# Block-sparse attention followed by a rational feed-forward layer: the start of the program in another order, a scale of its own for the first chunk, and its sampled key blocks copied by VectorE

## The chip, the cores and the metric

The kernel runs on one core of a Trainium2 chip. The metric is the device time of one execution in microseconds (us). The kernel before took 877.2 us, the median of three runs (875.51 to 879.96).

## What is computed

```python
B, H, S, D = 4, 8, 768, 64            # q, k, v: float32
scores = (q @ k.T) / sqrt(D)          # per batch and head
# a block of 32 queries sees the key blocks: itself and its two neighbours, block 0, block 23,
# and three sampled blocks (sampled_blocks, 24 x 3); blocks 0 and 23 as queries see all
attn = softmax(where(mask, scores, -1e9)) @ v
x = attn.transpose(0, 2, 1, 3).reshape(B * S, H * D)      # 3072 x 512
h = x @ w_in                                              # 3072 x 2048
P = a[0] + a[1]*h + a[2]*h**2 + a[3]*h**3
Q = 1 + abs(b[0])*abs(h) + abs(b[1])*h**2
out = (P / (Q + 1e-6)) @ w_out                            # 3072 x 512
```

The two weights come as float64 and are unpacked on the chip. q and k, and x and `w_in`, are multiplied in float16 as a high and a low part, each after a scale by a power of two that is found from the largest absolute value.

## The kernel before

**Two halves that run into each other.** Attention works by query blocks of 32 rows (function `attention`, "parts" numbered x; a query block that sees all keys has three parts). One part is: scores on TensorE (PE, L913), maxima on VectorE (DVE, L923), exponentials on ScalarE (ACT, L941), transposes on PE (L982) and their copy out of PSUM (`pT`, L150), products with v on PE (L1039). Four parts make a group: it is weighted (`xn`, L1073), turned (L1085, `xt`), and split into a high part `xh` (`evac_high`, L150 under `times`) and a low part `xl` (L1097). Eight query blocks make a chunk c of 256 rows of x; there are 12 chunks. The feed-forward half works by units (c, u), 8 per chunk: products with `w_in` (L1150 to L1152), the rational function on ACT and DVE, and products with `w_out` (L1206 to L1208). A unit needs its chunk's `xh` and `xl`, and the piece of the weights that it reads.

**The weights.** `weights` loads 16 tiles of `w_in` and 16 of `w_out` of 512 KB through two buffers (`wl`, L435 and L438). Each is converted (L154 or L150) and packed by DVE in three steps (L447, L450, L453). Four tiles make one group of `w_in`: ACT finds the largest value of each (L397), `w_scaled` makes the scale `scw`, and POOL (GpSimd) and ACT make the float16 parts (L154, L150, L511). A group serves two units.

**The first batch.** Its keys lie in SBUF (`kall`). `prep(0, ...)` loads k, bounds it (L397), splits it (L391), turns it on PE and evacuates it into `kall` (L150, L152); it also loads all of v for the bound that gives `v_scale[0]` and `kv[0][4]`, the factor by which x of batch 0 is scaled. For each part with samples, ACT copies three blocks of `kall` to `kx` (L866), at positions that it reads into registers with `TENSOR_LOAD` (L803): one such load brings the numbers of up to four query blocks, three each. SP (SyncE), which issues all DMAs, does the same for the rows of v (L1009). POOL copies the edge blocks into `kx` once (L1109). `prep_q` loads and splits four blocks' queries (`ldq`, L728).

**The order.** A planner (`issue`) places every operation by hand-set priorities and prices and by rings of buffers; each engine then runs its own list strictly in that order, so that an instruction that waits holds up all that stand behind it. Where PE would be idle early on, the planner adds products of the identity that nothing reads (`fill`, L162).

```python
lambda w, stage, j: (-83.96, -78.19)[w] + stage * 0.5                    # when(0): k first, then v
a = Op(SC, 1100, copies, [o_setup, chain["edges"]], p - 1, takes=[s_kx], uses=s_kall)
times(eng, x_part(0), G["xt"], kv[b][4] if plain else 1.0)              # x of a chunk, by v's scale
```

Of the kernel before, what the change touches and what calls it, by code (L numbers as in the profile page):

```python
# [23 lines left out]
def kernel(  # L24
# [265 lines left out]
    ix = const.tile([1, NB, 4], I32, name="ix")  # L290

# [122 lines left out]
    def weights():  # L414
# [5 lines left out]
        for u in range(NG):  # L420
            pieces += [(min(place[0, 2 * u], place[1, 2 * u]) + -4.91, 0, u, x) for x in range(NCC)]
# [131 lines left out]
    def prep(b, when):  # L553


        kv[b] = [None] * 5
        s_scr[b] = Slot(r_ks)
        first = b == 0
        n = len(units)
        k_done[b], v_done[b] = [], []  # L560
        before = {}
        if first:
            rings = [[(r_tt, "tt", p2), (r_ab, "ab", p2), (r_sq, "sq", p2)], [(r_pr, "pr", p3), (r_ld, "ld", p3)]]
        for w in ([2] if b >= QB else []) + [0, 1]:
# [7 lines left out]
            for j in range(n):  # L572
                def one(j, w=w, lds=lds, mx_tile=mx_tile):
                    prio = when(w, 0, j)
                    if first:
                        ring, tag, pool = rings[w][j // (2 + w)]
                    else:
                        ring = r_ld
# [6 lines left out]
                    def load():  # L585
                        if first:
                            nb = {"tt": 3, "pr": 4}.get(tag)
                            d["ld"] = pool.tile([P, 512], F32, name=tag, bufs=nb)
                            if w:
                                nc.sync.dma_start(out=d["ld"], in_=v[b].rearrange("h (a r) d -> (h a) (r d)", a=P // H)[:, j * 512:(j + 1) * 512])  # L590
                            else:
                                load_unit(k, b, *units[j], d["ld"])
# [120 lines left out]
    def prep_q(b, t, prio, before):  # L713
# [4 lines left out]
        s_ld, s_hl, s_ps = Slot(r_ldq), Slot(r_hlq), Slot(r_sp)  # L718
# [4 lines left out]
        def load():  # L723
            d["ld"] = p1.tile([P, 512], F32, name="ldq")
# [58 lines left out]
        x = Op(TE, 445, transposes, [l], prio, takes=[s_ps], uses=[s_hl])  # L783
        x = Op(SC, 904, evac, [x], prio, takes=[d["slot"]], uses=[s_ps])
# [12 lines left out]
    def sampled_rows(x, eng=mybir.EngineType.SP):  # L797

        b, j = parts[x][:2]
        i = block(j)  # L800
        if (b, i, eng) not in rows_of:
            some = [n for n in (block(m) for m in range(j - j % 4, j - j % 4 + 4)) if n not in (0, NB - 1)]
            values = nc.values_load_multi_w_load_instructions(  # L803
                ix[0:1, some[0]:some[-1] + 1, 0:NR], engines=[eng], min_val=0, max_val=NB - 1,
                skip_runtime_bounds_check_because="clamped when ix was written")[1]
            for n, m in enumerate(some):
                rows_of[b, m, eng] = values[n * NR:(n + 1) * NR]
        return rows_of[b, i, eng]
# [19 lines left out]
    xs_of, s_xs, o_ready = {}, {}, {}  # L828
# [4 lines left out]
    def attention(b, j, prio):  # L833
# [8 lines left out]
        if e4 == 0:  # L842
            x_group[w] = {"s_xn": Slot(r_xn), "s_ps": Slot(r_sp), "s_sm": Slot(r_sm), "ops": [], "av": []}
# [5 lines left out]
        for m, x in enumerate(xs):  # L849
            def one(m, x):  # L850
# [9 lines left out]
                elif near:  # L860
                    s_kx = Slot(r_kx)

                    def copies():
                        rows = sampled_rows(x, mybir.EngineType.Activation)
# [104 lines left out]
        for m, x in enumerate(xs):  # L969
            def two(m, x):  # L970
# [72 lines left out]
                ol = chain["vg"] = Op(SY, price, load, [o_setup] + v_done[b],  # L1043
# [36 lines left out]
        s_xn, s_ps = G["s_xn"], G["s_ps"]  # L1080

        def turn_x():
            G["xt"] = ps_s.tile([P, 512], F32, name="sp")
            for e in range(XB):
                nc.tensor.transpose(G["xt"][:, e * P:(e + 1) * P], G["xn"][:, e].rearrange("p g d -> p (g d)"), ident)  # L1085

# [3 lines left out]
        def evac_high(eng):  # L1090
            if c not in xs_of:
                xs_of[c] = xbufs[s_xs[c].buf]
            times(eng, x_part(0), G["xt"], kv[b][4] if plain else 1.0)

        def evac_low():
            if plain:
                nc.vector.scalar_tensor_tensor(out=x_part(1), in0=G["xt"], scalar=kv[b][4], in1=x_part(0), op0=ALU.mult, op1=ALU.subtract)  # L1097
            else:
                nc.vector.tensor_tensor(out=x_part(1), in0=G["xt"], in1=x_part(0), op=ALU.subtract)

        a = chain["xt"] = Op(TE, 435, turn_x, G["ops"], p, takes=[s_ps], uses=[s_xn], behind=chain.get("xt"))
        new = e2 < XB
        a = chain["ev"] = Op(among("v", SC, sc=520, ve=598), 0, evac_high, [a] + ([v_scale[b]] if plain else []), p, behind=chain.get("ev"), takes=[s_xs[c]] if new else [], uses=[s_ps] + ([] if new else [s_xs[c]]))
# [7 lines left out]
    last_near = []  # L1111
    XB = 4
# [4 lines left out]

    def factors(b, u, n, after, prio):

        def run():  # L1120
            if b not in fcs:
                fcs[b] = p2.tile([P, 4, NU], F32, name="fc")
            nc.vector.scalar_tensor_tensor(out=fcs[b][:, :, u:u + n], in0=wscale[:, u:u + n].rearrange("p (o n) -> p o n", o=1).broadcast_to([P, 4, n]), scalar=kv[b][3],
# [9 lines left out]
    def unit(c, u):  # L1133
# [6 lines left out]
        def into(e):  # L1140
            def run():
                xh, xl = xs_of[c]
                d["cst"] = fcs[b][:, :, u]
# [80 lines left out]
        deps = (o_ready[c] + [o_fc[b, u]] if u == 0 else [o_fc[b, u]]) + (in_ready[u * CH // WC] if c < 2 else [])  # L1224
# [81 lines left out]
    def when(b):  # L1306
        if b == 0:
            return lambda w, stage, j: (-83.96, -78.19)[w] + stage * 0.5
# [4 lines left out]
    prep(0, when(0))  # L1313
# [3 lines left out]
    for b in range(B):  # L1317
        if b:
            prep(b, when(b))
        for t in range(NT):  # L1320
            x0 = min(x for x, p in enumerate(parts) if p[0] == b and p[1] // TB == t)
            before = prep_q(b, t, -78.95 if b == t == 0 else part_prio(x0) - (3.23 if x0 >= need[0] else 12.17), before)
# [4 lines left out]
    for c, u in order:  # L1327
        b = c // NCH
        if b == 0 and u % (WC // CH) == 0 and (b, u) not in o_fc:
            factors(0, u, WC // CH, [scale_ready[u * CH // WC], v_scale[0], o_setup], place[c, u] - 1)  # L1330
        elif b and (b, u) not in o_fc:
# [45 lines left out]
```

## Time and profile before

| | |
|---|---|
| median of three runs | 877.2 us (875.51 to 879.96) |
| the profiled execution: its own time | 878.83 us |
| its span, first to last instruction | 877.0 us |
| PE, DVE, ACT, POOL busy | 825.4, 729.0, 675.4, 111.4 us |
| mean granted TensorE clock | 0.976 of full speed |
| moved by DMA | 151.16 MB, 172 GB/s over the span |

Read it by stages, not by the shares: PE's 825.4 us contain the `fill` products of the start, and the bound is not the same engine throughout. "Idle before" is the time in which an engine had nothing running, put down to the instruction that then came and to what released it. Register instructions such as `TENSOR_LOAD` are not counted as busy, so an engine that is held by them looks idle.

### The profile page before, as it was taken

Reading aid. Unit: us, or ns where it says so; the run is one execution under the profiler, and the core shown is the slowest. Engines: PE = TensorE matmul, PEld = TensorE weight load, DVE = VectorE, ACT = ScalarE, POOL = GpSimd, SP = SyncE. Lnnn points to the kernel's source line nnn. Section 1 sums busy time; section 2 is a strip of 40 time slices with the busy share of each in tenths; the row PEclk is TensorE's granted clock in tenths of the full one; section 3 lists DMA queues with packets and bytes.
Section 4 is the critical chain, followed back from the end, with each engine's and each line's share of the span. In section 5 each row is a group of like instructions: output and inputs, shape, how many; then the busy total and the mean of one; then the engine's idle time right before and its main releaser. Section 6 shows DMA issues by size and latency. Waiting matters only on the chain.

```text
span 877.0 us, 27047 instructions
## 1 busy us (share of the span) xinstructions
PE 825.4 (94%) x10334; PEld 644.6 (73%) x10334; DVE 729.0 (83%) x1731; ACT 675.4 (77%) x1447; POOL 111.4 (13%) x118
## 2 busy tenths in 40 slices
PE   8988687588899999999999999999999999999997
PEld 3545566366687888888788887878778888788886
DVE  5758987999998888888887877887878887778886
ACT  6777977797787897798777788998768687767563
POOL 1124622635220000000000000000000000000000
PEclk9999898699999999999999999999999999999999
DMA  7888689586765965889755976899555965630000
GB/s 201 209 158 209 194 177 199 127 238 196 203 156 152 273 203 157 210 214 241 200 146 139 241 204 190 198 248 248 152 131 162 224 170 160 183 102 26 1 25 25
DMA packets 240209, 151.16 MB, mean 172 GB/s; under 512 B 16208, under 2 KB 222928, under 8 KB 240080
## 3 DMA queue, kind: packets, MB, share of 16 engines
q1 hardware_dynamic: 240080, 149.43, 66.4%
q8 instruction: 82, 1.34, 0.7%
q14 instruction: 47, 0.39, 0.2%
HBM read 132.07 MB, written 11.01 MB: 163 GB/s over the span
## 4 chain that ended last, share of the span: by engine, by line
PE 69%; DVE 9%; DMA 9%; ACT 5%; SPq 4%; issue 3%; POOL 1%; ACTq 0%; DVEq 0%; POOLq 0%
PE acc L1206 9%; PE ph L1150 9%; PE acc L1208 8%; PE acc L1207 8%; PE ph L1152 8%; PE ph L1151 8%; PE av L1039 5%; PE pt L982 5%; PE sp L913 5%; DMA vg<-in_v_dram 2%; DMA wl<-in_moe_w_in_dram 2%; ACT pr L941 1%; DVE pr L923 1%; SPq L1009 1%; PE sp L758 1%
## 5 line engine op out<-in xcount | busy, mean ns | idle before, releaser
L1150 PE MATMUL ph<-xh,wi 128*128 128x256 f16 x768 | 212.1, 276 | 3.7 <-DVE tt L1167 3.6
L1152 PE MATMUL ph<-xh,wi 128*128 128x256 f16 x768 | 210.9, 275 | 0.5 <-POOL wi L511 0.5
L1151 PE MATMUL ph<-xl,wi 128*128 128x256 f16 x768 | 210.9, 275 | 0.0
L1206 PE MATMUL acc<-wo_h,gh 128*128 128x512 f32 x376 | 161.2, 429 | 1.4 <-ACT wo_h L150 1.4
L1208 PE MATMUL acc<-wo_h,gl 128*128 128x512 f32 x376 | 151.2, 402 | 2.6 <-DVE gl L1195 2.6
L1207 PE MATMUL acc<-wo_l,gh 128*128 128x512 f32 x376 | 150.5, 400 | 1.5 <-POOL wo_l L464 1.5
L1174 DVE SCALAR_TENSOR_TENSOR ab<-sq,absb,ab 128x512 f32<-128x512 f32 x96 | 73.0, 760 | 51.4 <-ACT ab L1171 51.2
L1157 ACT ACTIVATE sq<-ph,fc 128x512 f32<-128x512 f32 x96 | 65.7, 684 | 63.8 <-PE ph L1152 63.3
L1150 PEld LDWEIGHTS <-wi 128*128 128x128 f16 x768 | 75.7, 99 | 28.8 <-issue 16.3
L923 DVE CUSTOM_DVE_ANT_1 pr<-sp,bias 128x256 f32<-128x256 f32 x224 | 84.6, 418 | 13.3 <-PE sp L913 11.5
L941 ACT ACTIVATE pr<-pr,st,cqb 128x256 f32<-128x256 f32 x112 | 66.1, 593 | 29.1 <-DVE st L952 29.0
L1208 PEld LDWEIGHTS acc<-wo_h,gl 128*128 128x128 f32 x376 | 71.9, 191 | 20.3 <-DVE gl L1195 3.0
L1206 PEld LDWEIGHTS acc<-wo_h,gh 128*128 128x128 f32 x376 | 72.2, 192 | 17.8 <-ACT wo_h L150 1.6
L1185 DVE SCALAR_TENSOR_TENSOR gh<-tt,par,rr 128x512 fp32r<-128x512 f32 x96 | 73.2, 763 | 13.9 <-PE acc L1207 11.2
L982 PE MATMUL pt<-ident,pr 128*128 128x128 f32 x448 | 76.5, 292 | 8.6 <-ACT pr L941 6.9
L1151 PEld LDWEIGHTS <-wi 128*128 128x128 f16 x768 | 75.7, 99 | 11.7 <-issue 3.8
L1039 PE MATMUL av<-vg,pT 128*32 128x64 f32 x3584 | 74.1, 224 | 10.2 <-DMA vg<-in_v_dram 6.2
L1152 PEld LDWEIGHTS <-wi 128*128 128x128 f16 x768 | 75.7, 99 | 10.3 <-POOL wi L511 1.0
L982 PEld LDWEIGHTS pt<-ident,pr 128*128 128x128 f32 x448 | 67.7, 205 | 20.2 <-ACT pr L941 10.1
L1207 PEld LDWEIGHTS acc<-wo_l,gh 128*128 128x128 f32 x376 | 72.3, 192 | 13.8 <-POOL wo_l L464 1.8
L1039 PEld LDWEIGHTS av<-vg,pT 128*32 128x32 f32 x3584 | 56.3, 111 | 35.2 <-issue 15.3
L150 ACT ACTIVATE pT<-pt 128x512 f32<-128x512 f32 x112 | 66.3, 592 | 15.3 <-PE pt L982 13.6
(167 smaller groups left out, 1663.3 us busy)
## 6 DMA issues: line engine op xcount, KB each, us to landing
vg<-in_v_dram SPq DMA_DIRECT2D x312, 64.0 KB, 3.3
vg<-in_v_dram SPq DMA_DIRECT2D x88, 192.0 KB, 3.7
vg<-in_v_dram SPq DMA_DIRECT2D x24, 512.0 KB, 5.5
kall<-ks SPq DMA_DIRECT2D x52, 192.0 KB, 3.3
kall<-ks SPq DMA_DIRECT2D x156, 64.0 KB, 2.2
ld<-in_k_dram SPq DMA_DIRECT2D x36, 256.0 KB, 4.5
wl<-in_moe_w_in_dram SPq DMA_DIRECT2D x32, 256.0 KB, 4.5
wl<-in_moe_w_out_dram SPq DMA_DIRECT2D x16, 512.0 KB, 5.0
```

Source lines behind the costliest of these rows:

```text
L923: nc.vector.tensor_tensor_reduce(out=prs[x][:, g].rearrange("p (s r) -> p s r", r=BLK), in0=h["sp"][:, g].rearrange("p (s r) -> p s r", r= ...
L941: nc.scalar.activation(out=prs[x][:, g], in_=prs[x][:, g], func=AF.Exp, scale=Q["first"]["c"], bias=st[:, 6 + g:7 + g], accum_out=total if ...
L982: nc.tensor.transpose(pp[:, jj * P:(jj + 1) * P], cols, ident)
L1039: nc.tensor.matmul(av[rows, g], pT[:, 2 * g + kt, rows] if plain else pT[:, 2 * g + kt, pa_, rows], vf[:, g * HG + h4, kt * D:(kt + 1) * D ...
L1150: nc.tensor.matmul(o, wh, xh[:, :, cc], start=(cc == 0), stop=False)
L1151: nc.tensor.matmul(o, wh, xl[:, :, cc], start=False, stop=False)
L1152: nc.tensor.matmul(o, wl, xh[:, :, cc], start=False, stop=(cc == NCC - 1))
L1174: nc.vector.scalar_tensor_tensor(out=d["ab"], in0=d["sq"], scalar=absb[:, 1:2], in1=d["ab"], op0=ALU.mult, op1=ALU.add)
L1185: nc.vector.scalar_tensor_tensor(out=d["gh"], in0=d["tt"], scalar=par[:, 0:1], in1=d["rr"], op0=ALU.add, op1=ALU.mult)
L1206: nc.tensor.matmul(acc[:, t], ghs, wo_h[:, f], start=(new and e == 0), stop=False)
L1207: nc.tensor.matmul(acc[:, t], ghs, wo_l[:, f], start=False, stop=False)
L1208: nc.tensor.matmul(acc[:, t], gls, wo_h[:, f], start=False, stop=(last and e == 1))
```

## The change

Six edits, made together:

- **Loads.** v of batch 0 is no longer loaded right after k. Its priority goes from -78.19 to -7.0, and it stands behind the v rows of the last part of chunk 0. The second piece of q is loaded right after the first (it takes a buffer of another ring for that), and the first group of `w_in` gets priority -60.
- **The scale of chunk 0.** x of chunk 0 waits for v's bound no more. Both groups of it stay in PSUM (in the `ph` ring) while ACT finds each one's largest value; a scale `scx` is made of them (one more transpose on PE and five small steps on DVE), and both are then split. Chunk 0 gets its own unit factors (`fc`).
- **The copies of chunk 0.** The sampled blocks of the first eight parts are copied by DVE, those of the other 14 parts of batch 0 by ACT as before.
- **Reading the positions.** The three numbers of a query block are packed into one by DVE at the start; each part loads that one number and takes it apart with register instructions. This holds for all parts, on SP too.
- **Prices** in the planner's table: 700 for three copies on DVE, 1500 on ACT (1100 before); one slot of the q ring is taken earlier.
- Later chunks keep v's scale.

```diff
+        for r in range(NR - 1, 0, -1):
+            nc.vector.scalar_tensor_tensor(out=ix[:, :, NR:NR + 1] if r == 1 else ix[:, :, r - 1:r], in0=ix[:, :, r:r + 1], scalar=float(1 << IXB), in1=ix[:, :, r - 1:r], op0=ALU.mult, op1=ALU.add)
...
-            pieces += [(min(place[0, 2 * u], place[1, 2 * u]) + -4.91, 0, u, x) for x in range(NCC)]
+            pieces += [((min(place[0, 2 * u], place[1, 2 * u]) + -4.91) if u else -60.0, 0, u, x) for x in range(NCC)]
...
+        before = dict.fromkeys(range(3), vg_load.get(need[0] - 1)) if b < 2 else {}
...
-        s_ld, s_hl, s_ps = Slot(r_ldq), Slot(r_hlq), Slot(r_sp)
+        s_ld, s_hl, s_ps = Slot(r_ld if (b, t) == (0, 1) else r_ldq), Slot(r_hlq), Slot(r_sp)
...
-        if (b, i, eng) not in rows_of:
-            some = [n for n in (block(m) for m in range(j - j % 4, j - j % 4 + 4)) if n not in (0, NB - 1)]
...
+        if (x, eng) not in rows_of:
+            n = nc.values_load_multi_w_load_instructions(
+                ix[0:1, block(parts[x][1]), NR:NR + 1], engines=[eng], min_val=0, max_val=(1 << NR * IXB) - 1,
...
+            rows_of[x, eng] = [nc.s_assert_within((n >> r * IXB) & ((1 << IXB) - 1), min_val=0, max_val=NB - 1,
...
-                            nc.scalar.copy(out=kxs[:, s_kx.buf, r].rearrange("p h r -> p (h r)"), in_=kall[:, bass.ds(rows[r], 1)].rearrange("p o h r -> p (o h r)"))
+                            times(nc.vector if dve else nc.scalar, kxs[:, s_kx.buf, r].rearrange("p h r -> p (h r)"), kall[:, bass.ds(rows[r], 1)].rearrange("p o h r -> p (o h r)"), 1.0)
...
-                    a = Op(SC, 1100, copies, [o_setup, chain["edges"]], p - 1, takes=[s_kx], uses=s_kall)
+                    a = Op(VE if dve else SC, 700 if dve else 1500, copies, [o_setup, chain["edges"]], p - 1, takes=[s_kx], uses=s_kall, behind=chain.get("kx"))
...
+        def most():
+            if not x_own:
+                x_own.extend([p4.tile([P, 8], F32, name="mx", bufs=5), p4.tile([P, 1], F32, name="xs0", bufs=1)])
+            bound(G["xt"], x_own[0][:, e2 // XB:e2 // XB + 1])
...
+        o = Op(VE, 75, largest, [w[3] for w in x_wait], p)
+        o, _ = scales(lambda: x_own[0][:, 6:7], "scx", [o], p, finish=keep, keep=lambda s, inv: x_own.append(inv))
+        x_scaled.append(o)
+        for G, e2, p, _ in x_wait:
+            evacuate(G, c, e2, p, x_own, 1, o)
...
-            return lambda w, stage, j: (-83.96, -78.19)[w] + stage * 0.5
+            return lambda w, stage, j: (-83.96, -7.0)[w] + stage * 0.5
...
-            before = prep_q(b, t, -78.95 if b == t == 0 else part_prio(x0) - (3.23 if x0 >= need[0] else 12.17), before)
+            before = prep_q(b, t, -78.95 + 8 * t if b == 0 and t < 2 else part_prio(x0) - (3.23 if x0 >= need[0] else 12.17), before)
```

How the lists move, at three places. First the DMA queue of SP after the last loads of k; `ldq` and `ld` take q, `pr` and `ld` took v, `wl` takes weights, `vg` the v rows of part 0. Before:

```order
L545 DMA sq<-in_k_dram 128x4x128 x2
L728 DMA ldq<-in_q_dram 64x4x128 x2
L590 DMA pr<-in_v_dram 128x512 x3
L590 DMA ld<-in_v_dram 128x512 x3
L1003 DMA vg_110<-in_v_dram 48x8x128
```

and now:

```order
L548 DMA sq<-in_k_dram 128x4x128 x2
L728 DMA ldq<-in_q_dram 64x4x128 x2
L728 DMA ld<-in_q_dram 64x4x128 x2
L441 DMA wl<-in_moe_w_in_dram 64x1024 x4
L1001 DMA vg_110<-in_v_dram 48x8x128
```

The six loads of v have gone from here (they come after the v rows of part 7), and the second piece of q and two tiles of weights stand in their place.

Second, DVE's list just ahead of the first maxima (the ISA rows on `pr,st`). Before:

```order
L365 TENSOR_SCALAR scq<-scq 128x1
L746 SCALAR_TENSOR_TENSOR cq<-scq,sc_259 128x1
L749 TENSOR_SCALAR cq<-cq 128x1
L752 TENSOR_SCALAR cq<-cq 128x1
L391 SCALAR_TENSOR_TENSOR hlq<-ldq,scq,hlq 128x8x64
L923 ISA pr,st<-sp,bias 128x256
```

and now:

```order
L450 TENSOR_SCALAR wi<-wi 128x512
L752 TENSOR_SCALAR cq<-cq 128x1
L453 SCALAR_TENSOR_TENSOR wi<-wl,wi 128x512
L800 TENSOR_LOAD ix
L152 REGISTER_ALU
L152 ISA
L152 COPY kx<-kall 128x256
L152 REGISTER_ALU x2
```

Packing of weights (`wi`) has come ahead of the first maxima, and so have the copies of parts 0 and 1, each part with a load, five register operations, three ISA rows and three copies.

Third, DVE's list where chunk 0's second group is weighted (`xn`) and split (`xl`). Before:

```order
L1073 TENSOR_TENSOR xn<-av,sm 128x512
L749 TENSOR_SCALAR cq<-cq 128x1
L752 TENSOR_SCALAR cq<-cq 128x1
L154 TENSOR_SCALAR wi<-wl 128x512
L447 TENSOR_SCALAR wi<-wi 128x512
L1097 SCALAR_TENSOR_TENSOR xl_116<-sp,xscale,xh_115 128x512
```

and now:

```order
L1071 TENSOR_TENSOR xn<-av,sm 128x512
L1094 TENSOR_REDUCE mx<-mx 128x1
L356 TENSOR_REDUCE scx<-sp 128x1
L359 TENSOR_SCALAR scx<-scx 128x1
L368 TENSOR_SCALAR scx<-scx 128x1
L1097 COPY xs_1066<-scx 128x1
L1152 SCALAR_TENSOR_TENSOR fc<-wscale,scx,coef 128x4x2
L450 TENSOR_SCALAR wi<-wi 128x512
L453 SCALAR_TENSOR_TENSOR wi<-wl,wi 128x512
L1125 SCALAR_TENSOR_TENSOR xl_116<-ph,xs_1066,xh_115 128x512 x2
```

Between weighting and splitting there is now the making of a scale (two of its rows, L363 and L367, are left out here), and both groups are split together.

## Rows read from the trace of the kernel before

**Rows 1.** The span in 40 equal slices of 21.9 us: busy tenths of PE and of DVE (9 is 90% or more).

```profile
PE   8988687588899999999999999999999999999997
...
DVE  5758987999998888888887877887878887778886
```

**Rows 2.** Stretches between 12 and 250 us: length, busy time (and count) of PE, weight loads, DVE, ACT and POOL, granted clock, DMA share, GB/s.

```profile
12.20:30.40 18.20, 17.46 (x151) 9.35 (x152) 14.07 (x43) 13.70 (x32) 5.25 (x8) 1.00 0.68 186
30.40:60.00 29.60, 24.76 (x514) 14.97 (x517) 18.67 (x64) 24.59 (x72) 2.72 (x4) 1.00 0.95 200
60.00:75.00 15.00, 14.71 (x139) 8.34 (x139) 11.46 (x25) 10.06 (x24) 9.57 (x10) 0.89 0.89 175
75.00:100.00 25.00, 18.48 (x355) 12.11 (x352) 21.66 (x64) 21.67 (x54) 14.32 (x13) 1.00 0.70 204
100.00:160.00 60.00, 45.37 (x753) 35.93 (x753) 50.71 (x132) 46.95 (x114) 19.86 (x20) 0.85 0.81 178
160.00:210.00 50.00, 39.83 (x437) 30.86 (x437) 50.00 (x106) 44.55 (x98) 25.84 (x23) 0.84 0.76 202
210.00:250.00 40.00, 34.00 (x452) 26.95 (x452) 39.51 (x93) 29.67 (x61) 12.86 (x12) 0.96 0.70 183
```

**Rows 3.** The `TENSOR_LOAD` of positions (L803): duration in ns (shortest, median, longest), first and last start. The first two rows are of the whole span, the third of 42 to 55 us (a load of twelve numbers), the last of 55 to 75 us (a load of nine: one of the four query blocks has no samples).

```profile
L803 SPq TENSOR_LOAD <-ix x24: 1907/2529/2726, 13.8 to 739.9; - x24
L803 ACTq TENSOR_LOAD <-ix x6: 1991/2659/2836, 25.2 to 151.8; - x6
...
L803 SPq TENSOR_LOAD <-ix x1: 2552/2552/2552, 43.8 to 43.8; - x1
...
L803 SPq TENSOR_LOAD <-ix x1: 1911/1911/1911, 60.4 to 60.4; - x1
```

**Rows 4.** The copies on ACT and their register instructions (L866): duration in ns (shortest, median, longest), first and last start.

```profile
L866 ACTq FUSED_REGOPS  x66: 46/46/52, 28.1 to 157.9; - x66
L866 ACT COPY kx<-kall x66: 386/400/410, 28.2 to 161.1; 128x256 f16 x66
```

**Rows 5.** Groups of DVE and ACT instructions in the first 300 us: line, engine, operation, tiles, shape, count, busy us, mean ns, idle before and its releasers.

```profile
L93 DVE CAST ident<-ident 128x128 f16<-128x128 f32 x1 | 0.2, 227 | 1.4 <-POOL ident masks.py:199 1.4
L333 DVE TENSOR_SCALAR bias<-rr 128x24 f32<-128x24 f32 x3 | 0.3, 184 | 0.1
L152 DVE COPY kall<-ph 128x512 f16<-128x512 f16 x6 | 4.1, 712 | 0.2 <-ACT kall L150 0.2
L353 DVE TENSOR_REDUCE scw<-sp 128x1 f32<-128x128 f32 x4 | 1.1, 284 | 0.1
L356 DVE TENSOR_SCALAR scw<-scw 128x1 f32<-128x1 f32 x4 | 0.6, 143 | 0.0
L1123 DVE SCALAR_TENSOR_TENSOR fc<-wscale,sc,coef 128x8 f32<-128x8 f32 x4 | 1.5, 364 | 0.0
L397 ACT ACTIVATE scrap<-ldq 128x512 f16<-128x512 f32 x10 | 6.3, 629 | 1.7 <-DMA ldq<-in_q_dram 1.7
```

**Rows 6.** The start in order of time: start us, duration us, engine, line, operation, tiles, shape, count, idle before.

```profile
25.23 0.73 ACT L150 ACTIVATE kall<-ph 128x512 f16<-128x512 f16 x1 [0.57 <-PE ph L683]
26.79 1.16 POOL L1109 COPY kx<-kall 128x512 f16<-128x512 f16 x2 [4.74 <-DVE kall L152]
28.23 1.94 ACT L866 COPY kx<-kall 128x256 f16 x6 [2.27 <-DVE cq L752]
29.77 0.23 PE L913 MATMUL sp<-kall,qa 128*32 128x96 f16 x4
...
59.91 0.91 PE L1039 MATMUL av<-vg,pT 128*32 128x64 f32 x32 [3.48 <-DMA vg<-in_v_dram]
61.71 2.03 POOL L154 TENSOR_SCALAR dw<-wi,scw 128x512 f32<-128x512 f32 x3 [12.43 <-DVE scw L365]
66.64 0.74 DVE L1097 SCALAR_TENSOR_TENSOR xl<-sp,xscale,xh 128x512 f16<-128x512 f32 x1
71.21 1.32 POOL L511 TENSOR_TENSOR wi<-dw,wi 128x512 f16<-128x512 f32 x1 [0.23 <-ACT wi L150]
72.47 0.27 PE L1150 MATMUL ph<-xh,wi 128*128 128x256 f16 x1
```

**Rows 7.** Whom DVE waited for: waiting instruction, releaser, us in total, times, longest. The first three rows are of 30.5 to 60 us, the other three of 100 to 160 us.

```profile
DVE wi L447 <- ACT wi L150: 3.3, 1, 3.3
DVE pr L923 <- PE sp L913: 3.0, 3, 1.3
DVE pr L923 <- ACT kx L866: 1.6, 1, 1.6
...
DVE wi L447 <- POOL wi L154: 3.0, 3, 2.0
DVE sums L490 <- ACT scrap L397: 1.8, 1, 1.8
DVE dw L447 <- POOL dw L154: 1.3, 2, 0.8
```

**Rows 8.** The chain that ended last, in order of time, three of its long pieces between 121 and 153 us: start us, length us, what.

```profile
121.13 4.84 DMA wl<-in_moe_w_in_dram
125.98 6.15 DMA wl<-in_moe_w_in_dram
...
144.58 7.48 DMA wl<-in_moe_w_out_dram
```

More of the change, by code (lines that the diff above doesn't have):

```diff
@@ L574, in one @@
                     prio = when(w, 0, j)
-                    if first:
-                        ring, tag, pool = rings[w][j // (2 + w)]
+                    if first and w == 0:
+                        ring, tag, pool = rings[j // 2]
                     else:
@@ L585, in load @@
                     def load():
[L586 to L592, printed above, removed]
+                        if first and w == 0:
+                            d["ld"] = pool.tile([P, 512], F32, name=tag, bufs=3 if tag == "tt" else None)
+                            load_unit(k, b, *units[j], d["ld"])
                         else:
@@ L782, in prep_q @@
             d["first"], d["oc"] = qt[b, 0], qt[b, 0]["oc"]
-        x = Op(TE, 445, transposes, [l], prio, takes=[s_ps], uses=[s_hl])
-        x = Op(SC, 904, evac, [x], prio, takes=[d["slot"]], uses=[s_ps])
+        x = Op(TE, 445, transposes, [l], prio, takes=[s_ps, d["slot"]], uses=[s_hl])
+        x = Op(SC, 904, evac, [x], prio, uses=[s_ps, d["slot"]])
         d["oq"] = Op(SY, [(650, 131072)] * 2, swap, [x], prio, uses=[d["slot"]])
@@ L797, in sampled_rows @@
     def sampled_rows(x, eng=mybir.EngineType.SP):
-        b, j = parts[x][:2]
-        i = block(j)
-        if (b, i, eng) not in rows_of:
-            some = [n for n in (block(m) for m in range(j - j % 4, j - j % 4 + 4)) if n not in (0, NB - 1)]
[L803 to L808, printed above, removed]
+        if (x, eng) not in rows_of:
+            n = nc.values_load_multi_w_load_instructions(
+                ix[0:1, block(parts[x][1]), NR:NR + 1], engines=[eng], min_val=0, max_val=(1 << NR * IXB) - 1,
+                skip_runtime_bounds_check_because="made of numbers clamped when ix was written")[1][0]
+            rows_of[x, eng] = [nc.s_assert_within((n >> r * IXB) & ((1 << IXB) - 1), min_val=0, max_val=NB - 1,
+                                                  skip_runtime_bounds_check_because="clamped when ix was written") for r in range(NR)]
+        return rows_of[x, eng]
     def vrows(vg, kt, slot, n=1):
@@ L1041, in values @@
                                                  start=(n_ == 0 and (n == 1 or (m == 0 and g == 0))), stop=(m == n - 1 and n_ == len(steps) - 1), skip_group_check=n > 1)
-                ol = chain["vg"] = Op(SY, price, load, [o_setup] + v_done[b],
+                ol = chain["vg"] = vg_load[x] = Op(SY, price, load, [o_setup] + v_done[b],
                                       prio[m] - 0.72, takes=[s_vg], uses=[] if plain else [s_scr[b]], behind=chain.get("vg"))
@@ L1092, in evac_high @@
                 xs_of[c] = xbufs[s_xs[c].buf]
-            times(eng, x_part(0), G["xt"], kv[b][4] if plain else 1.0)
+            times(eng, x_part(0), G["xt"], of[n])
         def evac_low():
[L1096 to L1101, printed above, removed]
+            nc.vector.scalar_tensor_tensor(out=x_part(1), in0=G["xt"], scalar=of[n], in1=x_part(0), op0=ALU.mult, op1=ALU.subtract)
         new = e2 < XB
-        a = chain["ev"] = Op(among("v", SC, sc=520, ve=598), 0, evac_high, [a] + ([v_scale[b]] if plain else []), p, behind=chain.get("ev"), takes=[s_xs[c]] if new else [], uses=[s_ps] + ([] if new else [s_xs[c]]))
+        a = chain["ev"] = Op(among("v", SC, sc=520, ve=598), 0, evac_high, [G["turned"], ready], p, behind=chain.get("ev"), takes=[s_xs[c]] if new else [], uses=[s_ps] + ([] if new else [s_xs[c]]))
         l = Op(VE, 602, evac_low, [a], p, uses=[s_ps, s_xs[c]])
@@ L1327 @@
     for c, u in order:
[L1328 to L1331, printed above, removed]
+        b = key(c)
+        if c < 2 and u % (WC // CH) == 0:
+            factors(b, u, WC // CH, [scale_ready[u * CH // WC], v_scale[0] if c else x_scaled[0], o_setup], place[c, u] - 1)
+        elif b > 0 and (b, u) not in o_fc:
             factors(b, 0, NU, [scale_ready[g] for g in range(NG)] + [v_scale[b]], place[c, u] - 2)
```

62 lines of the change are left out of this document (42 added, 20 removed).

## Prediction

> **What bounds the kernel now.** I read the slices first, to see where time is lost. After slice 12 PE shows nines to its last slice; all gaps lie in the first 250 us [rows 1]. In those 250 us the digits of PE also count products that nothing reads, so that I go on by DVE. The stretches show it [rows 2]: between 160 and 250 us DVE is busy for 89.5 of 90 us while PE has 16.2 us idle, so there DVE is the bound. From 12 to 160 us DVE is idle for 31.5 us: 4.1, 10.9, 3.5, 3.3 and 9.3 us, stretch by stretch (length less busy time). DVE's work up to the point at which PE takes over is nearly fixed: splits, packing of weights, maxima, the first units. So the rule for the sum is: **the end moves by what DVE's early work grows, less what is taken out of DVE's idle time before 160 us.** PE is full afterwards and keeps the shift.
>
> Next, who made DVE wait [rows 7]. Between 30 and 60 us it is a conversion of weights that waits for its load and holds up DVE's list (3.3 us), scores (3.0 us) and ACT's copies (1.6 us). Between 100 and 160 us it is conversions and bounds of weights once more, and the long pieces of the chain there are loads of weights of 4.84, 6.15 and 7.48 us [rows 8]: the two `wl` buffers circulate too slowly.
>
> Last, the start in order of time [rows 6]. Keys are in place for POOL's edge copy at 26.79 us, ACT's copies begin at 28.23, the first scores at 29.77. Chunk 0's last `xl` starts at 66.64, but the first unit starts at 72.47, right after the last float16 part of the weights (POOL, 71.21 + 1.32): now weights end last there, not x.
>
> **The change part by part.**
>
> *Register loads.* A load of twelve numbers took 2.55 us, one of nine 1.91 us [rows 3]: 0.21 us for a number, and next to nothing beside it. One number then costs some 0.27 us. To it come five register operations and three address instructions of about 0.046 us each, by the nearest register row [rows 4], 0.37 us: 0.64 us for a part. The load may also have a fixed part that two sizes don't show; the ends are 0.2 us and 1.91 us, the shortest that ran. I take 0.27, since the two sizes lie on a line through nearly zero. The Trainium skill, "DMA: Bandwidth & Descriptors", section "Latency and other measured facts", gives a floor of about 600 ns for a `tensor_load`. By it the eight parts on DVE would cost 2.6 us more in all (8 x 0.33) and the forecast would be near 875; no run so far shows a load of one number, and the straight line of the measured ones speaks against it.
>
> *ACT.* It loses 24 copies of 0.40 us [rows 4], 9.6 us, and its six loads of 1.99 to 2.84 us, some 14.6 us in all (two of nine numbers, four of twelve), against 14 x 0.64 = 9.0 us now. It gains two bounds of some 0.63 us [rows 5]. ACT gets about 14 us freer before 160 us. It is not the bound there, so by itself this buys nothing; it shortens the waits that DVE has for ACT.
>
> *SP.* Its 24 long loads (55.8 us: 16 of 2.53 and 8 of 1.91) become 88 short ones, one per part with samples, of 0.64 us with what follows them: 56.3 us. The sum stays, but no single stop of 2.5 us holds up the queue. One such stop can be named: at 59.91 PE had waited 3.48 us for v rows [rows 6]. It was hidden, since the weights came later, so I price SP at nothing.
>
> *DVE, what is added.* 24 copies of 128 x 256 in float16. The trace has none on DVE from SBUF; below lies a small operation of 0.184 us, above half of the 0.712 us of a 128 x 512 evacuation, 0.36 us [rows 5]. I take 0.227 us, the cast of 128 x 128, the nearest in source and type: 5.5 us (4.4 to 8.5). Eight times 0.64 us of register work, 5.1 us; but a load runs beside the instruction ahead of it (ACT's started at 25.2 while its evacuation of 25.23 to 25.96 still ran [rows 3, 6]), so I take 3.0 us (0 to 5.1). The scale of chunk 0: one reduction of 0.284, seven small steps of 0.143 and its four unit factors of 0.364 [rows 5], 2.7 us, and two packing steps at the start, 0.3 us. Together **+11.5 us** (7.4 to 16.6).
>
> *DVE, what idle time goes.* (a) 12 to 30 us: v's reduction and its wait go, and packing of the first two weight tiles fills the gaps; of 4.1 us I expect 1 left: -3. This packing and the later split of the second q stand between the splits of k, three steps of 0.7 us. So the keys come about 2 us later, and first scores start near 32 us; that is work moved, not added. (b) 30 to 75 us, 14.4 us idle: the 3.3 us behind the late weight load and the 1.6 us behind ACT's copies go, of the other 9.5 us half (the list now has more ready work). Against it stands a new wait for x's own bound: ACT's bound (0.63), a reduction, a transpose, five small steps, then two `xh`, of which packing covers all but 3 us. Net -6.5. (c) 75 to 160 us, 12.6 us idle: with one weight group begun 20 us earlier and 14 us less on ACT, the 7.3 us of waits on weights and their bounds [rows 7] should mostly go: -7. Together **-16.5 us** (-5 to -22).
>
> *Loads of v.* 6 x 256 KB move from before 20 us to after the v rows of part 7. At the 175 GB/s of 60 to 75 us [rows 2] that is 9 us of DMA beside weight loads. In exchange 1 MB of weights left the stretch. I price it at nothing while the weights that units 0 to 3 need are already in; if they are not, up to 9 us fall on the chain of rows 8.
>
> **The sum.** +11.5 - 16.5 = -5 us. From the profiled execution's own 878.8 us this gives 873.8; that execution was 1.6 us above the median of the runs shown, so **872 us** against 877.2. From the ends of the terms alone: 7.4 - 22 to 16.6 - 5, -15 to +12.
>
> **Rivals.**
>
> *The waits change hands (877 us).* The first unit no longer waits for weights but for x: the edits on DVE make parts 0 to 7 later, then comes the serial chain of x's own scale. By hand along the new lists I get the first unit some 5 us later than 72.47, with five more packing pairs done. For it: DVE's list is already denser than ACT's in those stretches and gets 11.5 us more. Against: what is packed early is missing later. Then the -16.5 shrinks to -11.5: no change.
>
> *DVE carries it all to the end (884 us, slower).* One mechanism: DVE is the bound from 160 to 250 us with 0.5 us idle [rows 2], so each us of copies and register work that finds no idle time counts fully. If only (a) and the two named waits of (b) go, 3 + 4.9 less 3 for x's chain, about -5, and 11.5 stand against it: +6.5. It decides from 11.5 us on: less idle removed than that is a loss. (Loads of one number that took 1.91 us would do the same from the other side: 8 x 1.64 = 13 us more on DVE, 885 us; I give that little.)
>
> *v collides with weights (881 us).* The 1.5 MB come while `wl` circulates, and all 9 us lie on the chain: 872 + 9. For it speaks that loads of weights stand on the chain at all [rows 8]; against it, that it is the release of the two buffers and not the rate (175 GB/s, with 200 in the stretch before) that spaces them.
>
> *The start gains more (864 us).* The copies cost 0.184 us or less, register work hides fully (7.4 instead of 11.5), and idle time falls by 20 us: -13.
>
> **How the numbers follow.** The forecast case, 868 to 876, has 0.40; no change 0.24; DVE carries it 0.18; v collides 0.06; more gain 0.12. The range from 862 to 885 leaves out the far end of the gain and most of the dear loads. Faster or slower means by more than 0.5%, 4.4 us, about what a measurement of this kernel can tell from no change; the limits are 872.8 and 881.6. Faster: 0.26 of the forecast case, all of "more gain" and 0.02 of "no change", 0.40. Slower: "DVE carries it" 0.17, half of "v collides", 0.04 from "no change", 0.24. Same: the rest, 0.36.
>
> **What would show it.** The load of one number: near 0.27 us. DVE's copies to `kx`: near 0.23 us each. First scores near 32 us, the first unit between 70 and 78 us. DVE idle from 12 to 160 us: near 15 us instead of 31.5. DVE busy without a gap until PE takes over, some 5 us earlier than now. The prediction is wrong if DVE's idle time there stays above 20 us, if its list waits for x's own bound for more than 5 us, or if PE's idle time from 160 us on grows.

## The result, and the profile after

**The change made the kernel slower by 0.6%, where 0.6% faster was forecast.** Median 885.28 us (875.97 to 888.55, 13 executions) against 877.5 us (875.11 to 879.96, 13 executions); ratio 1.0062, 95% interval 1.0039 to 1.0084. The profiled execution took 888.55 us (span 886.8), the slowest of the 13; a second profile of the same kernel follows below (e12). Ratios leave out executions more than 1.5% above the fastest of the same kernel, which touches e12 alone: three of its twelve.

I follow both traces by *milestones*: milestone n is the start of the n-th write of `gl`, one for each unit (L1195 before, L1224 in the change). The difference of these starts, change less before, in us:

| unit | 1 | 5 | 15 | 20 | 31 | 43 | 45 | 59 | 67 | 71 | 96 |
|---|---|---|---|---|---|---|---|---|---|---|---|
| starts before at | 98.3 | 168.9 | 265.1 | 301.7 | 393.6 | 484.4 | 498.8 | 615.9 | 675.5 | 704.8 | 869.7 |
| change | +5.4 | -19.9 | -7.5 | **-7.7** | -4.7 | -4.0 | +2.3 | +4.8 | +3.1 | **+9.6** | **+9.8** |

By unit 20 the start has gained 7.7 us, more than the 5 us forecast. The loss of 17.5 us comes after 300 us, where I had expected nothing. The stretches that answer to [rows 2], of the change (columns as there):

```profile
12.20:30.40 18.20, 17.85 (x171) 10.21 (x175) 17.27 (x51) 12.36 (x22) 6.52 (x7) 1.00 0.73 174
30.40:60.00 29.60, 24.64 (x492) 14.85 (x489) 23.96 (x91) 21.23 (x60) 10.44 (x10) 0.91 0.68 150
60.00:75.00 15.00, 14.64 (x174) 9.21 (x172) 8.95 (x31) 11.39 (x28) 1.63 (x3) 0.94 1.12 269
75.00:100.00 25.00, 21.33 (x440) 15.10 (x437) 22.89 (x79) 23.18 (x59) 16.35 (x17) 1.00 0.95 243
100.00:160.00 60.00, 45.16 (x717) 35.92 (x721) 58.44 (x128) 51.69 (x121) 27.07 (x23) 0.91 0.87 197
```

DVE's idle time there (third pair, taken from the length) is 0.9, 5.6, 6.1, 2.1 and 1.6 us, together 16.3, where [rows 2] give 31.2. And the slices that answer to [rows 1], PE and its granted clock:

```profile
PE   8889786877999999999999799999999899999997
...
PEclk9999899988999999999999899999999899999999
```

The two digits under 9 behind the middle are new: PE's 7 and 8, each with an 8 of the granted clock under it, at 488 to 510 and 687 to 710 us. The waits of PE in the change, 250 to 500 us and then 500 to 700 us (line waited for, us in total, times, longest):

```profile
PE sp L758 <- DVE hlq L394: 4.6, 1, 4.6
PE av L1037 <- ACT pT L150: 1.9, 1, 1.9
...
PE sp L758 <- DVE hlq L394: 4.1, 1, 4.1
```

In the kernel before, no wait of PE after 250 us is longer than 0.4 us. The chain of work through the first of these stalls, in order of time:

```profile
487.95 6.89 DMA ldq<-in_q_dram
...
495.03 0.70 POOL hlq L154
...
495.76 0.76 DVE hlq L394
...
496.56 1.03 PE sp L758 x8
```

The first q piece of batch 2 lands at 494.9 us. POOL and DVE split it, and because DVE's list is in order, all of DVE stands still 7.2 us for it, then PE. The stretches around it show what a wait costs on top:

```profile
491.99:496.56 4.57, 0.01 (x1) 0.00 (x0) 0.80 (x2) 0.00 (x0) 0.69 (x1) 0.86 1.18 238
496.56:502.00 5.44, 5.44 (x68) 3.69 (x68) 5.22 (x12) 4.17 (x9) 0.00 (x0) 0.50 1.12 335
502.00:510.00 8.00, 8.00 (x102) 6.12 (x93) 5.68 (x18) 6.52 (x16) 1.77 (x1) 1.00 0.84 217
```

Having done nothing for 4.6 us, PE gets a granted clock of 0.50 (1.2 instead of 2.4 GHz) for the next 5.4 us. At half speed that would lose some 2.7 us more; 2.5 us were measured (see e1).

PE's wait for `pT`, the second row of its waits above, ended at 294.7 us and has the same root: ACT stands still for a q piece of batch 1, and `pT` comes behind it in ACT's list.

```profile
292.91 0.63 ACT L400 ACTIVATE scrap<-ldq 128x512 f16<-128x512 f32 x1 [3.19 <-DMA ldq<-in_q_dram]
```

Why was the load of batch 2 late? PE had been 4 us further ahead, but SP, which issues it, had not: it was issued at 486.65 us, and at 485.69 us in the kernel before. It also landed 7.8 us after its issue, not 5.9 us as before; these 1.9 us are not the list's. SP's own waits between 450 and 490 us, in the kernel before:

```profile
SPq L766 <- ACT qa L762: 5.2, 1, 5.2
SPq L728 <- DVE ab L1174: 1.6, 1, 1.6
SPq L728 <- DVE tt L1164: 0.7, 1, 0.7
SPq L1003 <- PE ph L1152: 0.4, 1, 0.4
SPq L1271 <- ACT pr L941: 0.4, 1, 0.4
```

and in the change:

```profile
SPq L728 <- DVE tt L1220: 1.2, 1, 1.2
SPq L1001 <- PE sp L911: 0.4, 1, 0.4
```

8.3 of 40 us before, 1.6 now: **SP's list has next to no slack left here.** From 250 to 690 us its waits fell from 55 to 42 us. What fills it is seen in the time of one part (keys and v of one query block). SP in the kernel before, start and length in us, with no load of positions in between:

```profile
443.20 0.38 SPq L1003 DMA_DIRECT2D vg<-in_v_dram  x1
443.77 1.35 SPq L1009 DMA_DIRECT2D vg<-in_v_dram  x3
445.18 0.42 SPq L880 DMA_DIRECT2D kall<-ks  x1
445.80 1.39 SPq L885 DMA_DIRECT2D kall<-ks  x3
447.30 0.37 SPq L1003 DMA_DIRECT2D vg<-in_v_dram  x1
```

and in the change, its load included:

```profile
440.62 0.42 SPq L878 DMA_DIRECT2D kall<-ks  x1
441.62 1.70 SPq L883 DMA_DIRECT2D kall<-ks  x3
443.42 0.38 SPq L1001 DMA_DIRECT2D vg<-in_v_dram  x1
444.06 1.65 SPq L1007 DMA_DIRECT2D vg<-in_v_dram  x3
445.75 0.42 SPq L878 DMA_DIRECT2D kall<-ks  x1
```

4.10 us a part before, to which a quarter of a load of 2.53 us comes, 4.73; in the change 5.13. That is 0.40 us a part, **26 us over the 66 parts with samples of batches 1 to 3** if all are like this one (60 of them are counted under e1). The keys' three transfers take 1.70 instead of 1.39 us, v's 1.65 instead of 1.35: the arithmetic that unpacks a number is done anew at each of the two places. Its rows in the change (duration in ns: shortest, median, longest; first and last start):

```profile
L883 SPq ALU_OP  x330: 32/37/48, 199.7 to 767.7; - x165
...
L1007 SPq ALU_OP  x440: 32/37/53, 14.4 to 777.8; - x147
```

770 such operations stand on SP, where there were none.

### The profile page after: what moved, and what is told of

Its sections match the earlier page's. It is cut to its first block, busy times and chain, and to the rows that moved or that the text cites. A ratio compares the mean times of both kernels' runs of the same rounds, so it can differ in the third digit from the quotient of the medians.

```text
span 886.8 us, 28018 instructions
## 1 busy us (share of the span) xinstructions
PE 829.1 (93%) x10327; PEld 645.2 (73%) x10327; DVE 735.7 (83%) x1768; ACT 668.5 (75%) x1427; POOL 120.7 (14%) x118
## 4 chain that ended last, share of the span: by engine, by line
PE 67%; DVE 16%; DMA 7%; ACT 3%; issue 3%; SPq 3%; POOL 2%; DVEq 0%; ACTq 0%; POOLq 0%
PE ph L1179 9%; PE acc L1235 8%; PE acc L1236 8%; PE acc L1237 8%; PE ph L1181 8%; PE ph L1180 8%; PE av L1037 5%; PE sp L911 5%; PE pt L980 4%; DMA vg<-in_v_dram 2%; DVE pr L921 2%; DMA ldq<-in_q_dram 1%; DVE tt L1193 1%; PE acc L162 1%; DVE gh L1214 1%
## 5 line engine op out<-in xcount | busy, mean ns | idle before, releaser
L1237 PE MATMUL acc<-wo_h,gl 128*128 128x512 f32 x376 | 149.4, 397 | 1.3 <-DVE gl L1224 1.3
L921 DVE CUSTOM_DVE_ANT_1 pr<-sp,bias 128x256 f32<-128x256 f32 x224 | 84.8, 418 | 11.8 <-PE sp L911 11.3
```

Source lines behind the costliest of these rows:

```text
L921: nc.vector.tensor_tensor_reduce(out=prs[x][:, g].rearrange("p (s r) -> p s r", r=BLK), in0=h["sp"][:, g].rearrange("p (s r) -> p s r", r= ...
L1237: nc.tensor.matmul(acc[:, t], gls, wo_h[:, f], start=False, stop=(last and e == 1))
```

## The experiments

**Theory S:** SP's list, lengthened by the register work, has no slack left in batches 1 to 3 and brings loads late. **Theory P:** SP's own work does not matter, PE has only run ahead of loads whose place in the order is fixed. **Theory D:** the start's gain is not real, DVE carries its new work to the end. Ratios are against the kernel before on the same chip; "u20" and "end" are the milestones of units 20 and 96 in the one profiled execution, in us against the trace before.

| run | median us | ratio (95%) | u20 | end |
|---|---|---|---|---|
| the change | 885.3 | 1.0062 (1.0039-1.0084) | -7.7 | +9.8 |
| e1: SP's loads grouped | 873.4 | 0.9927 (0.9905-0.9949) | -7.0 | -4.5 |
| e2: before, SP packed | 899.2 | 1.0220 (1.0186-1.0254) | -0.1 | +19.1 |
| e3: q early | 886.1 | 1.0075 (1.0046-1.0104) | -8.3 | +7.2 |
| e4: e1 and q early | 876.2 | 0.9954 (0.9927-0.9981) | -4.6 | +1.8 |
| e5: SP, three plain numbers | 875.6 | 0.9976 (0.9952-1.0000) | -9.1 | -7.6 |
| e6: e1, copies on ACT | 881.5 | 1.0048 (1.0027-1.0068) | -0.3 | +3.0 |
| e7: e1, first weights late | 881.2 | 1.0030 (1.0012-1.0048) | +0.7 | +2.2 |
| e8: e1, v's scale and early v | 885.0 | 1.0081 (1.0052-1.0110) | -1.7 | +6.0 |
| e9: change, swap on POOL | 873.6 | 0.9930 (0.9907-0.9953) | -6.7 | -6.5 |
| e10: e1, swap on POOL | 873.1 | 0.9924 (0.9903-0.9946) | -6.9 | -7.6 |
| e11: e1, swap on ACT | 908.0 | 1.0338 (1.0298-1.0378) | -5.9 | +24.3 |
| e12: the change again | 885.9 (883.8 of nine) | 1.0044 (1.0009-1.0079) | -7.0 | +5.0 |

e1 and e4 have the same lists up to 300 us and differ by 2.4 us at u20: smaller differences in that column say nothing.

**e1, the register work taken off SP alone.**

```diff
 def sampled_rows(x, eng=SP):
+    if eng == SP:
+        ...                       # as before: one load of up to 12 numbers for four blocks
+        return rows_of[b, i, eng]
     if (x, eng) not in rows_of:   # ACT and DVE: one packed number, as in the change
```

> The change as it is, but SP loads its row numbers as before (one load of up to twelve numbers for four parts, no register arithmetic); DVE and ACT keep the packed one-number loads, and the order of the work is untouched. Theory S (SP's 770 register operations and 88 loads fill its list between 250 and 690 us, so that the first q piece of batches 2 and 3 is issued late, POOL's and DVE's splits of it wait, and PE stands still twice): SP waits over 5 us between 450 and 490 us again (1.6 in the change, 8.3 before), PE's two waits for hlq of 4.6 and 4.1 us go, 871 to 875 us. Theory P (SP's own work is not the matter: PE has come 4 to 8 us forward and runs into loads that stand where they stood): the two waits stay, 882 to 886 us. Theory D (the gain of the start was never real and DVE carries it): 882 to 886 us, with no wait for hlq.

Measured 873.4 us: S. PE's only wait for `hlq` between 250 and 700 us is 0.3 us, and of the 7.0 us at u20 4.5 reach the end. SP waits 4.1 us between 450 and 490 us, less than the 5 that were expected. P and D fall with this run.

The lists of e1 and of the change hold the same work in the same order, so that PE's instructions can be compared one by one. The change is 1.6 us behind e1 just before its first stall, 6.4 behind it and 8.9 when the clock is back; at the second stall 7.8, 12.0 and 14.3. The two stalls and the slow clock after each make 13.8 of the 14.3 us between these two profiles. With its waits left out, SP's list takes 473 us in the change and 448 us in e1 for the same 709 transfers (60 of the 66 parts, 202 to 737 us in the change), 25 us more. The q piece of the first stall is issued at 480.13 us in e1, 6.5 us earlier than in the change:

```profile
480.13 1.97 SPq L728 DMA_DIRECT2D ldq<-in_q_dram  x2
```

**e2, the same work put on SP in the kernel before.** Here `sampled_rows` uses the packed number where `eng == SP`, and two steps of `setup` on DVE pack it; nothing else changes.

> The kernel before, with one part of the change alone: SP gets its row numbers from a packed number, one load and register arithmetic per part (two small DVE steps at the start pack them); ACT keeps the long loads. Theory S: SP's waiting between 450 and 490 us falls from 8.3 to under 4 us; PE is 4 us further back than in the change, so at most one of the two stalls shows; 879 to 885 us. Theory P: 876 to 879 us, no wait for hlq. Theory D: 876 to 879 us.

Measured 899.2 us, a loss of 2.2%: the sign and place are S's, the size was too low, as I had let the waits that SP has before absorb most of the 26 us. Units 10 to 20 agree with the trace before to 0.1 us; then the milestones fall back by 3.9 us at unit 21, 7.3 at 31, 11.3 at 45, 17.0 at 59 and 19.1 from 73 on. SP's waits from 450 to 490 us sum up to 1.1 us. PE's longer waits between 500 and 700 us are of three kinds, for q, v and keys that SP loads:

```profile
PE sp L761 <- DVE hlq L394: 2.3, 1, 2.3
PE av L1050 <- DMA vg<-in_v_dram: 2.3, 2, 1.7
PE sp L924 <- DMA xkg<-ks: 1.3, 1, 1.3
```

The start's -7.7 and e2's +19.1 make +11.4, near the +9.8 at which the change's first profile ended. Its second profile (e12) ended at +5.0, and by the medians taking this work off the change gives back 12 us (885.3 to 873.4): it costs less there than alone.

**e3 and e4, the q pieces of batches 2 and 3 some 10 us earlier** (`3.23` becomes `4.5` for `b >= QB`).

> The change as it is, but the q pieces of batches 2 and 3 stand 1.27 units (about 10 us) earlier in the order. Theories S and P: the late q load is what stops PE, so both waits for hlq go and the gain of the start reaches the end, 870 to 875 us. Theory D: 882 to 886 us. If another load of the same queue is late in its place, the time comes between, 876 to 881 us, and PE waits for that one at the same boundaries.

> Both edits together: SP's grouped loads and the q pieces of batches 2 and 3 some 10 us earlier. Theory S: no more than grouped loads alone give, 870 to 874 us. Theory P: as q early alone, 870 to 875 us. Theory D: 882 to 886 us.

Measured 886.1 and 876.2 us. Moving the late load forward on such a list bought nothing: the load was the place where the lateness showed, not its cause. The expectation named for e3 was wrong for S too; if SP has no slack, something else is late in its place (PE then waits 2.6 and 1.9 us for `pT` and still 2.3 us for `hlq`). e4 misses its 870 to 874 us too, and why is not shown: its profiled execution (880.6 us) is among its slowest, 2.4 us behind e1's at u20 and 6.3 at the end.

**e5, no arithmetic, but as many loads as in the change.**

```diff
-    n = values_load(ix[0:1, block(x), NR:NR + 1], ...)           # packed, then (n >> 5 r) & 31
+    rows_of[x, eng] = values_load(ix[0:1, block(x), 0:NR], ...)  # three plain numbers; SP only
```

> The change, but SP loads three plain numbers for each part, without arithmetic. By 0.21 us for a number a load should take 0.63 us, and SP's 88 loads 55.8 us in all, as the 24 long loads did. Theory S-sum (SP's list is too long by its sum: 10 register operations a part, done once for the keys and once for v): 872 to 876 us, like the grouped loads, and no wait for hlq over 1 us. Theory S-stops (it is the number of loads, 88 for 24, each a stop of the queue): 882 to 887 us, as the change.

Measured 875.6 us (871.2 to 879.8), inside S-sum. A load of three numbers took 0.68 us, so 88 of them are 59.6 us against 24 long loads of some 56:

```profile
L801 SPq TENSOR_LOAD <-ix x88: 663/677/1897, 13.9 to 746.3; - x88
```

It is less steady than e1, and on average worse (0.9976 to 0.9927), though its profiled execution ended 3 us ahead of e1's. Whether the rest is the 4 us of longer loads or the number of stops stays open; most of the loss went with the arithmetic.

**e9 and e10, SP's list shortened elsewhere.** The two copies from `qa` to `qc` of every q tile of batches 1 to 3 go to another engine's queue:

```diff
-nc.sync.dma_start(out=qc[D:], in_=qa[:D])
+(nc.gpsimd if b else nc.sync).dma_start(out=qc[D:], in_=qa[:D])   # the second copy likewise
```

> The change with its register work as it is; only the copies qa to qc of batches 1 to 3 (2 transfers for each of 18 tiles, 0.51 and 0.59 us of SP's list) are issued by POOL, which has nearly no work after 250 us; the order is untouched. Theory S-sum: SP's list gets some 20 us shorter from 250 us on, about what the change had added, so the time falls to 874 to 879 us and PE's waits for hlq shrink under 1.5 us, though no register operation is gone. If it is not the length of SP's list but something special to register arithmetic: 883 to 888 us. If issuing on POOL is dear or holds DVE up: over 886 us, with waits for POOL.

> Grouped loads on SP and those copies of qa issued by POOL. Theory S-sum: SP's list is some 20 us shorter than before the change; the start's gain of 7 us at unit 20 then reaches the end whole (with grouped loads alone 2.4 us of it were lost again): 869 to 873 us. If PE sets the pace by itself there: as grouped loads alone, 872 to 875 us.

e9 is the strongest of these runs: all 770 register operations are still there, 36 transfers are issued by POOL instead, and the time falls from 885 to 873.6 us, just below the 874 to 879 expected. Its milestones stay between -4.0 and -9.3 us from unit 20 to the end, and no wait of PE from 250 to 700 us is over 0.3 us. What the transfers cost on POOL (ns: shortest, median, longest):

```profile
L766 POOL DMA_DIRECT2D qc<-qa x18: 518/565/705, 203.0 to 731.1; - x18
L767 POOL DMA_DIRECT2D qc<-qa x18: 516/518/527, 203.7 to 731.6; - x18
```

So nothing special to register work is needed: other work taken off SP's list does as well. With the copies SP also loses its stops ahead of them (5.2 of its 42 us of waits in the change), and e9 does not tell these from the time to issue. e10 shows the other side: relieved by both, SP waits 23.5 us between 490 and 600 us (13.6 before), no wait of PE is listed from 250 to 700 us, the start's 6.9 us reach the end whole, and the time is that of e1 within the intervals. There PE sets the pace alone. e1, e9 and e10 are all 0.7 to 0.8% faster than the kernel before.

**e11, the same on ACT.**

```diff
 def evac():                       # ACT writes qa
     ...
+    if b: cross(nc.scalar)        # both copies, issued right behind it
```

> The same with ACT issuing the copies, right behind the evacuation that writes qa. SP is relieved as much; ACT gets some 1.2 us for each of 18 tiles, and its list stands while it waits for its own evacuation. Theory S-sum: 869 to 874 us, if ACT has room; if ACT's products (pT, the factors of the units) then come late, PE waits for ACT and the time is 875 to 880 us.

Measured 908.0 us, worse by far than expected. ACT around one such tile, and PE's waits for `pT` from 250 to 500 and from 500 to 700 us:

```profile
357.81 1.32 ACT L762 ACTIVATE qa<-sp 128x1024 f16<-128x1024 f16 x1 [0.15 <-PE sp L758]
364.83 0.50 ACTq L767 DMA_DIRECT2D qc<-qa  x1
366.72 0.47 ACTq L768 DMA_DIRECT2D qc<-qa  x1
367.24 0.60 ACT L150 ACTIVATE pT<-pt 128x512 f32<-128x512 f32 x1 [8.11 <-DMA ld<-in_k_dram]
...
PE av L1054 <- ACT pT L150: 10.3, 5, 6.7
...
PE av L1054 <- ACT pT L150: 11.7, 3, 6.3
```

Issuing the two copies takes 1.2 us of ACT's list where they can go at once, some 21 us for 18 tiles. Here ACT did nothing else for 8.1 us: each copy waited first for a transfer that SP had issued to land, and ACT's list behind it waited too. Over the 18 tiles ACT gives another 25 us, mostly to such waits. At three tiles they are 6.9, 5.6 and 3.3 us and stand ahead of PE's three longest waits for `pT`, of 6.7, 6.3 and 4.1 us, which are 17 of its 22.0 us; no wait of 1.2 us is seen at each tile. On POOL, from the end of `qa` to the end of the second issue, a tile took 1.3 to 2.0 us but for the first (4.7 us), and no wait of PE followed.

**e6, e7 and e8, the parts of the start undone one by one**, on top of e1: `dve = False` for the copies; `-60.0` taken back for the first weights; `(-83.96, -78.19)` in `when(0)`, with v's scale and `prep(0, when(0), [0, 1])` as before. The planner orders the start anew each time.

> Grouped loads on SP, and the copies of sampled key blocks of chunk 0 back on ACT (with the packed number); all else as in the change. If the prediction's rule holds as it stands (the end moves by DVE's early work, which shrinks by 5.5 to 8.5 us): unit 20 another 4 to 8 us earlier than with the copies on DVE, 865 to 870 us. If the copies on DVE are what took DVE's idle time out (its waits for ACT's copies and for scores): unit 20 some 2 to 6 us later, 875 to 880 us. If they only change places: within 1.5 us of 873.4.

> Grouped loads on SP, and the first weight group back in its old place in the order (30 to 60 us, not at the start). If early packing of weights is a main part of the gain of the start: DVE's idle time from 12 to 160 us rises by 3 to 8 us, unit 20 comes 3 to 8 us later, 876 to 881 us. If it is not: within 1.5 us of 873.4.

> Grouped loads on SP, chunk 0 scaled by v's maximum again and v loaded and reduced first, as before; copies on DVE and early weights as in the change. If moving v behind is a main part of the gain: unit 20 comes 3 to 7 us later, 876 to 880 us. If x's own scale costs as much (2.7 us of DVE and its serial chain) as v's late load brings: within 1.5 us of 873.4. If it costs more: 868 to 872 us.

Each alone takes the whole gain or most of it: u20 moves from -7.0 to -0.3, +0.7 and -1.7. The times are above the ranges named for this case, e6 and e7 just so (875 to 880, 876 to 881), e8 by 5 us (876 to 880). e8 loses another 7.7 us behind u20; 3.5 of them are a wait of PE for a bound on ACT at 360 us, the rest is open. DVE from 12.2 to 160 us in e1 (busy times in the order of [rows 2]; DVE is the third):

```profile
12.20:160.00 147.80, 123.41 (x1950) 84.52 (x1951) 130.92 (x376) 119.34 (x288) 61.60 (x57) 0.94 0.91 198
```

and in e6:

```profile
12.20:160.00 147.80, 124.00 (x1811) 81.64 (x1812) 120.60 (x338) 117.04 (x292) 59.63 (x62) 0.92 0.90 190
```

DVE is idle for 16.9 us there in e1 and for 27.2 us in e6 (24.3 and 23.3 us in e7 and e8). The rule of the prediction would have had e6 end earlier, as it takes some 8.5 us of work off DVE; it came 6.7 us later at u20. So the copies most likely stood on DVE in time in which it would have waited. In e6 DVE waits most from 12 to 75 us for POOL's conversion of weights, 10.3 us in all, against 3.4 in e1. The three edits therefore cannot be given a share each: as it seems, each fills gaps that the others would leave open, though part of the differences may come from the planner's other order.

**e12, the change once more.**

> The change once more, to see whether PE's two waits for hlq come in every execution: 880 to 887 us; an execution without the wait near 490 us, or with a short one, should be some 5 us faster than one with both.

Measured 885.9 us (877.0 to 891.2). In its profiled execution (883.8 us) PE waits for `hlq` for 0.4 us between 400 and 500 us and for 2.5 us between 600 and 700 us, and for `pT` for 3.2 us between 250 and 300 us; it ended 4.8 us ahead of the first profile. The load of the first stall was issued at the same time (486.77 us) but landed 5.8 us later instead of 7.8, and PE came to it 2.3 us later. The 3.2 us for `pT` follow 4.6 us in which ACT stands for a q piece. So the two long stalls are one form of the loss, not its law: with so little slack on SP, where PE runs into a late load, and for how long, changes from one execution to the next. The twelve executions of this run span 14.2 us, those of the kernel before beside them 8.7.

## Why the prediction was wrong

- **Prices of the loads and the copies: right.** A load of one number took 0.277 us on SP, 0.276 on ACT, 0.315 on DVE (0.27 forecast); the copy on DVE 0.227 us, as forecast:

```profile
L800 SPq TENSOR_LOAD <-ix x88: 263/277/1161, 13.8 to 766.0; - x88
L800 ACTq TENSOR_LOAD <-ix x14: 273/276/465, 48.0 to 172.5; - x14
L800 DVEq TENSOR_LOAD <-ix x8: 302/315/734, 26.9 to 45.1; - x8
...
L152 DVE COPY kx<-kall x24: 212/227/500, 27.9 to 46.2; 128x256 f16 x24
```

  The line through the two sizes of [rows 3] held. The Trainium skill gives a floor of some 600 ns for a `tensor_load` in "DMA: Bandwidth & Descriptors" ("Latency and other measured facts"); these rows show about half of it, and the measurement decides. The prediction's estimate from that floor, 2.6 us more on DVE, falls with it, and no part of the miss lies there.
- **The start: right in mechanism, near in size.** DVE idle from 12 to 160 us 16.3 us (forecast 15; before it was 31.2 by [rows 2], the prediction's 31.5 is a slip), first unit at 72.44 (70 to 78), u20 at -7.7 us (forecast -5). First scores came at 29.19 us, not near 32. The rule holds with measured terms: DVE's busy time in the whole span grew by 6.7 us (729.0 to 735.7), its idle time fell by 14.9, together -8.2 (register work counts as idle here). The new work was priced somewhat too high. Of the signs that were to prove it wrong, two did not come (DVE's idle time, and its wait for x's own bound, 1.9 us); the third did, PE's idle time later on. What was not right is the picture of terms that can be fixed one by one (e6 to e8): how much idle time goes depends on the work that is put there.
- **The step that failed: SP, priced at nothing.** "The sum stays": 0.64 us for each of 88 parts against 55.8 us. Two things were wrong in it. It counted the five register operations once for a part, but SP uses the numbers at two places in batches 1 to 3, for the keys and for v, and each place unpacks them again (770 operations, of which 660 in those batches). And it priced one by the length of a row, 0.046 us, where an operation on SP put the next transfer off by some 0.078 us. Ten operations at 0.046 us and a load of 0.27 make 0.73 us a part against 0.63 for a quarter of a long load, only 6.6 us in all over 66 parts; so the price is the larger part of the miss. (The three address instructions in the 0.64 had stood on SP before as well.) Measured: +0.40 us a part, 26 us. I had also asked of SP's stops only whether they hit the start.
- **"PE is full afterwards and keeps the shift": wrong because of it.** PE's nines in [rows 1] say that PE waited for nobody, not that its suppliers had room. By the sum the 26 us would have fitted: SP's waits from 250 to 690 us come to 55 us in the kernel before. But they do not lie where the work was added; in e2 SP still waits 41 us there, and 19 of the 26 us reach the end. With SP relieved the step holds: in e9 and e10 the shift of u20 stays to the end. With SP's loads as before (e1), the change gives 0.9927 of the kernel before; that is 871 us against the 872 forecast, though e1's profile loses 2.5 us of its start's 7.0 behind u20.
- **The rivals.** The end lies where "DVE carries it all to the end" put it (884 us), by another mechanism: DVE's new work did not reach the end. Of "v collides with weights" nothing is seen, with the start 7.7 us ahead. "The waits change hands" came in part: milestone 1 is 5.4 us later, but milestone 5 already 19.9 earlier.

## What to carry to other kernels

A bound that is hidden by another shows in no busy share: before adding to an engine that only issues transfers, take its time for one round of the loop (here 4.7 us with its share of a load) and its waits in the stretch where the round repeats (8 of 40 us), and ask how many rounds there are. Count an added register operation at each place that uses the value, not where it is written in the source, and price it by how far the next transfer moves, not by its row. Where one transfer comes late on such an engine, shorten its list, or give some of the issuing to an idle engine, rather than move that transfer forward. A busy engine is no place for it: a copy that must wait there holds up its whole list (e11).

## What was not expected of the hardware

- Register operations cost SP more than their rows say: two of 37 ns between transfers made each of these steps some 0.155 us longer ((1.70 - 1.39) / 2), 0.078 us for one.
- POOL issued a transfer in 0.52 to 0.57 us, with no wait of PE behind it; the same two transfers issued by ACT moved the end by 32 us (e10 to e11). Of these PE's waits for `pT` are 22.0 us from 250 to 700 us; the rest was not taken apart.
- A copy from SBUF to SBUF that ACT issued waited up to 5.6 us in ACT's list for a transfer issued by SP to land before it was issued itself (e11).
- A wait of PE of 4.6 us was followed by 5.4 us at half clock and cost 7.2 us in all (4.7 and 2.5, against the same instructions of e1).
